# Order of the first loads: columns 2 and 3 of x third, the index table behind the last columns

## Chip, core and metric

The kernel runs on one core of a Trainium2 chip. Its time is the device time of one execution in microseconds (us). Before the change it takes 178.44 us, the median of 9 runs (178.29 to 178.66).

## What is computed

The reference, cut to what matters:

```python
x  = A_x                                   # 1 x 2048 x 512, bf16
xn = layernorm(x)                          # over the 512
fft   = irfft2(rfft2(xn) * (w_r + 1j*w_i))
geglu = (gelu(xn @ w_gate) * (xn @ w_up)) @ w_down    # 512 -> 1792 -> 512
return x + fft + geglu
```

## The kernel before

**Tiling.** The 2048 rows lie as 16 "columns" of 128 rows: column c holds rows 16p + c for partition p. Four columns make a block. The gate and up weights (512 x 1792) lie as four slices of 128 inner rows, the middle width as 14 tiles of 128 (f = 0 to 13).

**Order of the work.** Matrix work on TensorE (PE) is one long list: a gate group and an up group (L490; the first gate group of all is L498) for each unit of columns and f, between them the matmuls of the Fourier part (L577, L635, L644, L738, L768), then the down projection (L817, L821). The order on each engine is fixed when the kernel is built. A planner (class `Plan`, L135 to L198) sorts the operations by estimated costs and landing times (the tables `LAND`, `WG_LAND`, `WU_LAND`, L308 to L312). The hardware then runs each engine's list strictly in that order, and an instruction waits for its inputs by semaphores.

**The first microseconds.** PE spins on zeros (L320). Columns 0 and 1 are normalized on VectorE (DVE) one by one (statistics L339 and L342, normalization L345) and transposed on PE (L351). Then come, in this order on PE: six more spin matmuls (L324), the gate group of column 0 for f 0 to 3 (L498, needs the first third of the gate weights `Wg_sb`), the transposes of column 1, the up group of column 0 (L490, needs the first third of the up weights `Wu_sb`), gate and up of column 1, the gate group of columns 0 and 1 for f 4 and 5 (needs the second part of `Wg_sb`), the transposes of columns 2 and 3, and so on. Columns 2 and 3 are normalized together on DVE and GpSimd (POOL, L357 to L361) after their statistics.

**The loads.** All plain loads are issued by SyncE (SP), one after the other, on one DMA queue, in the order of lines L281 to L306. `load_x(c0, n)` (L272) loads n columns, 128 KB each; `load_w(T, a, b)` (L275) loads the columns a to b of all four slices of one weight. The first thirds are 512 KB each, the last parts 768 KB each. The index table `idx_t` (L283, L284) is 128 rows of 12 bytes; it is read only by GpSimd's indirect loads (`gather`, L593) late in the Fourier part. Loads share eight semaphores in turn, so that from the ninth load on each waits until the load eight places before it has landed. Behind the loads in SP's list stand the DMA transposes of xn (L455), which feed the gate and up groups of blocks 1 to 3.

Of the kernel before, what the change touches and what calls it, by code (L numbers as in the profile page):

```python
# [201 lines left out]
def kernel(  # L202
# [11 lines left out]
    nc = tc.nc  # L214
    const_np, ccols, rf_np, ri_np, idx_np = _tables()
# [32 lines left out]
    def load_consts(first, last):  # L248
        a, b = ccols[first][0], sum(ccols[last])
        nc.sync.dma_start(out=CT[:, a:b], in_=cap[:, a:b])  # L250


    def load_x(c0, n, eng=nc.sync):
        eng.dma_start(out=x_t[:, c0:c0 + n, :], in_=x_v[:, c0:c0 + n, :])

    def load_w(a, b, eng=nc.sync):
        nc.sync.dma_start(out=Wg_sb[:, :, a:b], in_=wg_v[:, :, a:b])
        eng.dma_start(out=Wu_sb[:, :, a:b], in_=wu_v[:, :, a:b])
# [21 lines left out]
    pin(nc.scalar.activation(out=warm[:], in_=eps_t[:], func=AF.Sqrt, bias=eps_t[:], scale=1.0))  # L280
    pin(load_x(0, 1))  # L281
    pin(load_x(1, 1))
    idx_t = pc.tile([P, 3], I32, name="idx_t")  # L283
    nc.sync.dma_start(out=idx_t[:], in_=nc.inline_tensor(idx_np, name="spec_rows").ap())  # L284
    load_w(Wg_sb, 0, 512)
    load_w(Wu_sb, 0, 512)
    load_x(2, 2)
    load_w(Wg_sb, 512, 1024)
    load_w(Wu_sb, 512, 1024)
    load_x(4, 2)  # L290
# [6 lines left out]
        nc.sync.dma_start(out=RF_t[:, c:c + 8], in_=rf_d.rearrange("p (c k) -> p c k", c=NC)[:, c:c + 8])  # L297
    load_x(12, 2)
    load_x(14, 2)
    load_consts("F0", "L0")  # L300
    load_consts("I0", "M0")
    for T, w_in in ((TR, A_w_r), (TI, A_w_i)):
# [578 lines left out]
```

## Time and profile before

The profiled execution took 178.44 us, as long as the median of the nine runs. Its span, from the first to the last recorded instruction, is 176.7 us; the rest (1.7 us) lies around it.

| engine | busy us | share of the span |
|---|---|---|
| PE, matmul | 172.3 | 97% |
| PE, weight load | 96.4 | 55% |
| DVE | 116.0 | 66% |
| ACT | 95.9 | 54% |
| POOL | 17.2 | 10% |

The first loads, from the trace's DMA issues and landings (us from the start of the span):

| load, in order of issue | size | issued | landed |
|---|---|---|---|
| x column 0 | 128 KB | 0.80 | 2.94 |
| x column 1 | 128 KB | 1.24 | 3.43 |
| idx_t | 1.5 KB | 1.71 | 3.76 |
| Wg_sb, first third | 512 KB | 2.18 | 6.16 |
| Wu_sb, first third | 512 KB | 2.65 | 7.63 |
| x columns 2 and 3 | 256 KB | 3.20 | 8.39 |
| Wg_sb, second part | 512 KB | 3.75 | 10.11 |
| Wu_sb, second part | 512 KB | 4.23 | 11.60 |

How to read it: "issued" is the start of the instruction on SP's queue, "landed" the moment at which the last of the 16 DMA engines reports its share as written. An engine that is busy for most of the span sets the time; another engine's idle time costs nothing as long as the busy one doesn't wait for it.

### The profile page before, as it was taken

To read this page: it belongs to the slowest core of one execution; us is meant where nothing else is said; L and a number is where in the kernel's file an instruction comes from. 1 tells how busy PE (TensorE), PEld (TensorE's weight loads), DVE (VectorE), ACT (ScalarE), POOL (GpSimd) and SP (SyncE) were. 2 spreads that over 40 slices of the span, in tenths; PEclk is the share of its full clock that TensorE was granted. 3 is DMA by queue.
4 is the path that set the end of the run, shared out by engine and by line. 5 is a ranking of instruction groups with operands and counts; after the bars stand their busy time and mean duration, and the time that the engine had idled before them with its cause. 6 is when DMAs were issued, how large, how long until landed. Compare 5 with 4: busy or idle time off the path is not lost.

```text
span 176.7 us, 3132 instructions
## 1 busy us (share of the span) xinstructions
PE 172.3 (97%) x1145; PEld 96.4 (55%) x1145; DVE 116.0 (66%) x255; ACT 95.9 (54%) x170; POOL 17.2 (10%) x38
## 2 busy tenths in 40 slices
PE   7899999999999999999999999999999999999993
PEld 7698845455545554555555445454444445444463
DVE  3578999987334699979899999643516325345333
ACT  4442489799736988898899965362112111211200
POOL 1020340506760000000000000000000000000000
PEclk9999999999999999999999999999999999999999
DMA  3999999233718702211201510200122222221212
GB/s 91 360 374 379 368 187 151 59 70 67 254 31 270 268 0 59 59 30 35 59 24 37 152 46 15 59 0 4 59 89 89 80 72 61 89 89 60 82 40 59
DMA packets 21871, 19.35 MB, mean 109 GB/s; under 512 B 8480, under 2 KB 20000, under 8 KB 21856
## 3 DMA queue, kind: packets, MB, share of 16 engines
q1 hardware_dynamic: 21440, 17.84, 36.3%
q0 software_dynamic: 416, 1.32, 2.4%
q8 instruction: 9, 0.15, 0.3%
q14 instruction: 6, 0.05, 0.1%
HBM read 13.38 MB, written 2.10 MB: 88 GB/s over the span
## 4 chain that ended last, share of the span: by engine, by line
PE 94%; DMA 3%; SPq 1%; issue 0%; DVE 0%
PE u_ps L490 28%; PE y_ps L817 27%; PE g_ps L490 27%; DMA Wu_sb<-in_B_w_up_dram 3%; PE dp L635 2%; PE yp L768 2%; PE gp L738 2%; PE bp L577 2%; PE y_ps L821 2%; PE ep L644 2%; SPq L273 0%; PE tp L351 0%; SPq L277 0%; SPq L284 0%; DVE y_sb L824 0%
## 5 line engine op out<-in xcount | busy, mean ns | idle before, releaser
L490 PE MATMUL u_ps<-xnT,Wu_sb 128*128 128x512 bf16 (+2 forms) x272 | 57.3, 341 | 0.2 <-DMA Wu_sb<-in_B_w_up_dram 0.2
L490 PE MATMUL g_ps<-xnT,Wg_sb 128*128 128x512 bf16 (+2 forms) x256 | 56.2, 349 | 0.0
L817 PE MATMUL y_ps<-Wd_sb,hT 128*128 128x512 bf16 (+2 forms) x252 | 51.1, 355 | 0.0
L508 DVE TENSOR_TENSOR hT<-u_ps,ge 128x512 bf16<-128x512 f32 x56 | 38.4, 688 | 18.2 <-PE u_ps L490 14.6
L503 ACT ACTIVATE ge<-g_ps 128x512 bf16<-128x512 f32 x56 | 33.7, 601 | 24.2 <-PE g_ps L490 23.3
L490 PEld LDWEIGHTS <-Wu_sb 128*128 128x128 bf16 x272 | 24.9, 98 | 21.0 <-DMA Wu_sb<-in_B_w_up_dram 0.4
L817 PEld LDWEIGHTS <-hT 128*128 128x128 bf16 x252 | 23.2, 98 | 22.4
L490 PEld LDWEIGHTS <-Wg_sb 128*128 128x128 bf16 x256 | 24.0, 98 | 20.6
L774 ACT CAST yf<-yp 128x512 bf16<-128x512 f32 x16 | 9.3, 586 | 40.5 <-PE yp L768 40.5
L824 DVE TENSOR_TENSOR y_sb<-y_ps,y_sb 128x512 bf16<-128x512 f32 (+2 forms) x18 | 11.1, 631 | 30.1 <-PE y_ps L821 30.1
L649 ACT CAST E<-ep 64x512 bf16<-64x512 f32 x32 | 18.5, 579 | 1.4 <-PE ep L644 1.0
L339 DVE BATCH_NORM_STATS2 stats<-x_t 128x6 f32<-128x512 bf16 x16 | 10.3, 672 | 2.4 <-DMA x_t<-in_A_x_dram 2.4
L452 ACT ACTIVATE xn<-x_t,nb,rstd 128x512 bf16<-128x512 bf16 x12 | 9.5, 812 | 1.0 <-POOL nb L370 1.0
L547 ACT CAST ds<-dp 128x512 bf16<-128x512 f32 x16 | 9.2, 597 | 0.8 <-PE dp L635 0.8
L547 ACT CAST Gs<-gp 128x512 bf16<-128x512 f32 x16 | 8.7, 591 | 0.6 <-PE gp L738 0.5
L547 ACT CAST Bs<-bp 128x512 bf16<-128x512 f32 x16 | 8.3, 608 | 0.5 <-PE bp L577 0.5
L780 DVE TENSOR_TENSOR lv<-yf 128x512 bf16<-128x512 bf16 x16 | 6.1, 421 | 1.5 <-ACT yf L774 0.6
L768 PEld LDWEIGHTS <-Gs 128*128 128x128 bf16 x64 | 4.8, 98 | 3.5
L787 DVE TENSOR_TENSOR yt<-lv 128x512 bf16<-128x512 bf16 x16 | 6.1, 421 | 0.3
L821 PE MATMUL y_ps<-yt,RI_t 128*128 128x512 bf16 (+2 forms) x18 | 6.1, 355 | 0.0
L768 PE MATMUL yp<-CT,Gs 128*128 128x128 bf16 x64 | 6.0, 219 | 0.0
L559 DVE TENSOR_TENSOR A<-xn 128x1024 bf16<-128x1024 bf16 x8 | 5.2, 676 | 1.0 <-ACT xn L452 1.0
(65 smaller groups left out, 118.5 us busy)
## 6 DMA issues: line engine op xcount, KB each, us to landing
F<-F SPq DMA_DIRECT2D x32, 64.0 KB, 2.0
y_sb<-in_A_x_dram SPq DMA_DIRECT2D x16, 128.0 KB, 2.1
out_dram<-y_sb SPq DMA_DIRECT2D x15, 128.0 KB, 1.7
x_t<-in_A_x_dram SPq DMA_DIRECT2D x7, 256.0 KB, 8.7
Wd_sb<-in_B_w_down_dram SPq DMA_DIRECT2D x1, 1792.0 KB, 7.4
Wg_sb<-in_B_w_gate_dram SPq DMA_DIRECT2D x2, 512.0 KB, 5.2
Wu_sb<-in_B_w_up_dram SPq DMA_DIRECT2D x2, 512.0 KB, 6.2
Wg_sb<-in_B_w_gate_dram SPq DMA_DIRECT2D x1, 768.0 KB, 10.1
```

Source lines behind the costliest of these rows:

```text
L339: V.bn_stats(out=st[:], in_=x_t[:, c, :])
L452: xn_op[c] = add("ACT", 0.72, lambda c=c: A.activation(out=xn[:, c, :], in_=x_t[:, c, :], func=AF.Identity, bias=nb[:, c:c + 1], scale=rst ...
L490: T_.matmul(b[name][:, f], lhsT=W_[:, e, (f0 + f) * P:(f0 + f + 1) * P], rhs=rhs[:, e, :], start=(e == 0), stop=(e == NE - 1))
L503: A.activation(out=b["ge"][:], in_=b["g_ps"][:], func=AF.Gelu_apprx_tanh)
L508: V.tensor_tensor(out=hT_of(sb, f0, m, o, w), in0=b["u_ps"][:], in1=b["ge"][:], op=ALU.mult)
L547: A.copy(out=o, in_=i)
L649: A.copy(out=b["E"][64 * h:64 * h + 64, r], in_=b["ep", h][64 * r:64 * r + 64])
L768: T_.matmul(t[:, q], lhsT=late["G"][:, q, c0 + j], rhs=IQ[q], start=(q == 0), stop=(q == 3), skip_group_check=True)
L774: A.copy(out=b["yf"][:, j], in_=b[j][:])
L817: T_.matmul(b[o][:], lhsT=hT_of(sb, f, 1, cl * P, P)[:, 0], rhs=Wd_sb[:, f, o:o + w], start=(f == 0), stop=False)
L821: T_.matmul(b[o][:], lhsT=late["RI"][:, c, :], rhs=late["yt"][:, c, o:o + w], start=False, stop=True)
L824: V.tensor_tensor(out=b["y"][:, o:o + w], in0=b[o][:], in1=b["y"][:, o:o + w], op=ALU.add)
```

## The change

Two lines of the loading order move. No instruction of PE, DVE, ACT or POOL is added, removed or put in another place.

```diff
     pin(load_x(0, 1))
     pin(load_x(1, 1))
+    load_x(2, 2)
     idx_t = pc.tile([P, 3], I32, name="idx_t")
-    nc.sync.dma_start(out=idx_t[:], in_=nc.inline_tensor(idx_np, name="spec_rows").ap())
     load_w(Wg_sb, 0, 512)
     load_w(Wu_sb, 0, 512)
-    load_x(2, 2)
     load_w(Wg_sb, 512, 1024)
     load_w(Wu_sb, 512, 1024)
     load_x(4, 2)
...
     load_x(12, 2)
     load_x(14, 2)
+    nc.sync.dma_start(out=idx_t[:], in_=nc.inline_tensor(idx_np, name="spec_rows").ap())
     load_consts("F0", "L0")
```

So x columns 2 and 3 (256 KB) stand third in SP's list, ahead of the first thirds of both weights. Every load from the second Wg_sb part to x columns 14 and 15 moves up one place in the turn of the eight semaphores, and the index table stands between x columns 14 and 15 and the constants.

## Prediction

> **What bounds the kernel now.** I read the page's table of engines first, then the chain that ended last, then PE's waits, and last the DMA by stretches of time.
>
> ```profile
> PE 172.3 (97%) x1145; PEld 96.4 (55%) x1145; DVE 116.0 (66%) x255; ACT 95.9 (54%) x170; POOL 17.2 (10%) x38
> ```
>
> PE is busy for 172.3 of 176.7 us. The chain in order of time (start, length) says where the rest is:
>
> ```profile
> 1.24 0.42 SPq L273
> 1.71 0.42 SPq L284
> 2.18 0.43 SPq L277
> 2.65 4.98 DMA Wu_sb<-in_B_w_up_dram
> 7.68 1.07 PE u_ps L490 x16
> ```
>
> Up to 7.68 us the end is set by SP issuing loads one by one and by the landing of the first third of Wu_sb (2.65 + 4.98 = 7.63 us). From 7.68 us on it is PE alone. PE's waits, in full:
>
> ```profile
> PE sp_ps L320 <- DVE minus_half L266: 1.1, 1, 1.1
> PE g_ps L498 <- DVE xn L345: 0.3, 1, 0.3
> PE u_ps L490 <- DMA Wu_sb<-in_B_w_up_dram: 0.2, 1, 0.2
> ```
>
> After the third wait there is none: PE has no idle stretch over 15 ns between 7.68 and 174.0 us. So the time of this kernel is the start of the first up group plus a fixed length of matmuls, and **the change is worth what it does to the landing of two loads**: the first third of Wg_sb (6.16 us, used at 6.20) and of Wu_sb (7.63 us, used at 7.68). PE's gap ahead of 6.20 is put down to xn L345 in the row above, but the weight load of the same group is listed with 0.5 us of waiting for Wg_sb, which came last.
>
> **What the change removes: nothing from PE.** VectorE waits for the moved columns:
>
> ```profile
> 8.42 1.29 DVE L339 BATCH_NORM_STATS2 stats<-x_t 128x6 f32<-128x512 bf16 x2 [0.46 <-DMA x_t<-in_A_x_dram]
> 12.11 0.61 PE L351 MATMUL tp<-ident_t,xn 128*128 128x128 bf16 x8
> ```
>
> These statistics can start 0.47 us earlier, when the copy of column 1 ends (7.53 + 0.42 = 7.95 us). But PE comes to the transposes of columns 2 and 3 only at 12.0 us, straight from the gate group before them, without a gap. I cost this gain at 0; PE's own list hides it, and after it PE is still what is late.
>
> **What it moves on SP.** Third place on SP goes from the index table (issue 0.42 us) to a 256 KB load (0.50 us in its old place, 0.33 to 0.50 elsewhere), so Wg_sb is issued 0 to 0.1 us later. The delay from issue to the first packet is 1.03 us for x column 0 (0.80 to 1.83), 1.06 for the index table, 1.09 for Wg_sb (2.18 to 3.27): Wg_sb's descriptors would be ready at 3.3 to 3.4 us. That is not when they run, for the same queue then still holds the 256 KB.
>
> **What it moves on the DMA engines.** This is the term that decides. The columns are the stretch, its length, busy time (instructions) of PE, PEld, DVE, ACT and POOL, the clock, the busy share of the 16 DMA engines, and GB/s:
>
> ```profile
> 2.50:3.00 0.50, 0.50 (x8) 0.50 (x6) 0.04 (x1) 0.00 (x0) 0.00 (x0) 1.00 0.81 223
> 3.00:3.25 0.25, 0.25 (x5) 0.25 (x3) 0.25 (x1) 0.00 (x0) 0.00 (x0) 1.00 0.11 10
> 3.25:3.75 0.50, 0.50 (x8) 0.50 (x6) 0.47 (x2) 0.00 (x0) 0.00 (x0) 1.00 0.82 72
> 3.75:4.25 0.50, 0.50 (x8) 0.50 (x6) 0.50 (x2) 0.30 (x1) 0.00 (x0) 1.00 0.50 98
> 4.25:5.00 0.75, 0.63 (x10) 0.46 (x9) 0.71 (x5) 0.00 (x0) 0.00 (x0) 1.00 1.04 367
> ```
>
> There is a **hole from 3.0 to 4.25 us**. x columns 0 and 1 are through at 3.0; the index table fills its place in the queue with 1.5 KB; Wg_sb begins at 3.27 and runs slowly for a microsecond. 18 of its packets there take over 150 ns, the longest 851, where 46 is usual; then it reaches 367 GB/s. Moved in the hole: 0.25 x 10 + 0.5 x 72 + 0.5 x 98 = 88 kB; at 367 GB/s it would be 1.25 x 367 = 459 kB. So 371 kB, or 371 / 367 = 1.01 us of the queue, goes unused. The moved load is 262 kB, or 262 / 367 = 0.71 us. Its first packet would be there at 1.71 + 1.06 = 2.77 us, before x column 1 is through, so it runs in the hole.
>
> The bounds for the landing of the two first thirds:
>
> - Best: the hole is filled whole. +0.71 for the load, -1.01 for the hole: **-0.30 us**.
> - Hand-over kept: the queue already shows the moved load followed by a weight in the same layout, where the second Wg_sb part runs behind x columns 2 and 3:
>
> ```profile
> 7.00:7.50 0.50, 0.49 (x9) 0.32 (x6) 0.00 (x0) 0.20 (x1) 0.00 (x0) 1.00 0.99 340
> 7.50:8.25 0.75, 0.57 (x11) 0.58 (x12) 0.42 (x1) 0.40 (x1) 0.00 (x0) 1.00 1.05 317
> ```
>
>   Against 367 these lose 0.5 x 27 + 0.75 x 50 = 51 kB, or 0.14 us; there is no hole. So -0.30 + 0.14 = **-0.16 us**.
> - Slow start kept: if Wg_sb's slow microsecond is its own and comes whenever it starts, the load still covers only the part up to 3.25. Wg_sb starts at 3.0 + 0.71 = 3.71 instead of 3.25: **+0.46 us**.
> - Worst: the load itself brings no cover, and all its 0.71 us come on top: **+0.71 us**.
>
> I take **-0.2 us**, between the first two, because the nearest row is the same pair of loads in the same order; and the first third of Wu_sb, as cold as Wg_sb, shows no hole either where it starts behind a full queue (5.00 to 5.50 us: 358 GB/s). Even Wd_sb, which starts into idle engines at 53.7 us, has 297 GB/s in its second half microsecond. A slow microsecond belongs to none of them.
>
> The Trainium skill speaks against the change: "DMA: Bandwidth & Descriptors", section "Queues, rings and completion order", says that each DMA engine consumes the descriptors of a ring in order, so that whatever is put ahead of a weight must be started before it. By that rule taken alone the sum would be the size of the load over the rate, the last bound above; the trace's hole at 3.0 to 4.25 us is what the rule leaves out.
>
> **From landing to the end.** If Wu_sb lands 0.2 us earlier, PE's first up group starts 0.2 us earlier, if Wg_sb also comes in time: it lands earlier by about the same. PE's floor: the six spin matmuls end at 5.90, then 16 gate matmuls (0.91 us from 6.20 to the transposes at 7.11) and the transposes of column 1 (four at 56 ns, 0.22 us): 7.03 us. So no more than 7.68 - 7.03 = 0.65 us can be gained, whatever the loads do. Next on PE is the second part of Wg_sb (landed 10.11, used at 10.37). The bytes ahead of it are the same in both orders, less the hole, so it comes up to 1.0 us earlier and doesn't bind. A late start goes to the end in full, for PE has nowhere to make it up.
>
> **The rest costs nothing, with its cover.** The index table late: SP issues it behind x columns 14 and 15, which land at 22.77 now; it is first used at 41.8 us, about 17 us of cover. Its small packets may open a hole there as early on; 1.0 us at most, ahead of the constants and twiddle loads (used from 41.8 us) and the DMA transposes behind them. The transposes of block 1 land by 29.80, and PE uses them at 32.71: 2.9 us of cover. The semaphores' turn: the first transpose (22.06 us) now waits for x columns 14 and 15 (22.77) instead of 12 and 13 (21.62); it stood behind the twiddle loads in the queue anyway and landed at 27.44. The loads from the ninth on wait for other landings, one place earlier or later, while the engines are full (357 to 397 GB/s from 8.25 to 20 us), so their order of service stays. Each of these costs 0 unless its cover is gone.
>
> **Rivals.**
>
> 1. Hole filled, small gain (forecast): 178.44 - 0.2 = 178.2 us, own range -0.30 to 0 (178.1 to 178.4). Chance 0.50.
> 2. Larger gain: the 12-byte rows are what stalls Wg_sb, and what they did to the slower DMA engines goes too. Wg_sb's shares finish from 5.64 to 6.16 us; if this spread of 0.5 us shrinks by half, 0.25 is added to the 0.2: 178.0 us, at most 0.65 less (177.8). For it: the slow packets follow those rows directly and nothing else in the trace. Against it: Wu_sb's shares spread as far (7.13 to 7.63). Chance 0.22.
> 3. Slower, one mechanism: Wg_sb's slow start is its own, and the 256 KB ahead only push it back. +0.46 gives 178.9 us, up to 179.15 at the worst bound. It decides from the point where more than 0.30 us of the slow start remains. For it: nothing in the trace shows this first touch of Wg_sb behind a full queue. Against it: the three starts named above. Chance 0.20.
> 4. Cancel: part of the slow start is kept (some 0.3 us), 178.4 to 178.7 us. Or the hole closes, but the load's packets run at the 223 to 258 GB/s of x columns 0 and 1: 262 / 240 = 1.09 instead of 0.71 us, so -0.16 + 0.38 = +0.22. Chance 0.08.
>
> That the change does not do what it says is excluded for the order on SP, which is the program's order; that the earlier columns help no one is part of the forecast.
>
> **The numbers.** The profiled execution took 178.44 us, the median itself, so the sum is made on both: 178.2 us. What a measurement of this kernel can tell from no change is about 0.2%, or 0.36 us. Faster by more: rival 2 but for its smallest values, 0.22. Slower by more: rival 3 and a little of 4, 0.22. Within: 0.56. The range takes in rival 2 to -0.6 and rival 3 to +0.5: 177.85 to 178.95 us.
>
> **What the profile after would show.** If right: no stretch under 200 GB/s between 2.25 and 8 us; x columns 2 and 3 landed before 4.6 us; Wg_sb's first third at about 5.95 and Wu_sb's at about 7.4; the first L490 group at 7.45; PE without a gap after it; the first statistics of column 2 at about 7.7 to 7.95 with no DMA wait. Rival 2: Wu_sb before 7.2. Rival 3: the slow stretch again, at 3.7 to 4.7, and Wu_sb after 8.0. The forecast would be wrong altogether if PE shows new gaps after 7.7 us, at the use of Wg_sb's second part or at 32.7 us behind the transposes.

## The result and the profile after

The changed kernel takes **179.5 us** (median of 10 runs, 179.15 to 180.8), the kernel before 178.44 (median of 30 runs, 178.29 to 178.98): a ratio of 1.006, 95% interval 1.0048 to 1.0071. So it is 1.06 us slower; the forecast was 178.2 us. The profiled execution after took 179.56 us with a span of 177.9, 1.12 us more than the one before.

The page's line of engines after the change. PE's busy time is the same to 0.1 us, so nothing was added to PE's work:

```profile
PE 172.4 (97%) x1145; PEld 96.7 (54%) x1145; DVE 115.9 (65%) x255; ACT 95.9 (54%) x170; POOL 17.2 (10%) x38
```

The chain that ended last, after the change (start, length):

```profile
1.71 0.42 SPq L273
2.14 0.04 issue
2.18 0.43 SPq L277
2.61 0.04 issue
2.66 6.10 DMA Wu_sb<-in_B_w_up_dram
8.76 0.05 issue
8.80 1.07 PE u_ps L490 x16
```

It is the same chain. The issue of `Wu_sb` is where it was (2.66, before 2.65); from there to its landing it took 6.10 us instead of 4.98. The first up group starts at 8.80 instead of 7.68, and PE's last matmul at 174.87 instead of 173.74: +1.12 at the start, +1.13 at the end, and no gap between. PE's waits, all of them:

```profile
PE g_ps L498 <- DMA Wg_sb<-in_B_w_gate_dram: 1.4, 1, 1.4
PE sp_ps L320 <- DVE minus_half L266: 1.1, 1, 1.1
PE u_ps L490 <- DMA Wu_sb<-in_B_w_up_dram: 0.2, 1, 0.2
```

The new one is the first: PE stands 1.4 us before the first gate group, for the first third of `Wg_sb`. PE's list at this place, before (first three rows) and after (start, length; in brackets the idle time ahead of it):

```profile
6.20 1.07 PE L498 MATMUL g_ps<-xnT,Wg_sb 128*128 128x128 bf16 x16 [0.31 <-DVE xn L345]
7.11 0.39 PE L351 MATMUL tp<-ident_t,xn 128*128 128x128 bf16 x4
7.68 1.07 PE L490 MATMUL u_ps<-xnT,Wu_sb 128*128 128x128 bf16 x16 [0.19 <-DMA Wu_sb<-in_B_w_up_dram]
7.31 1.07 PE L498 MATMUL g_ps<-xnT,Wg_sb 128*128 128x128 bf16 x16 [1.40 <-DMA Wg_sb<-in_B_w_gate_dram]
8.21 0.39 PE L351 MATMUL tp<-ident_t,xn 128*128 128x128 bf16 x4
8.80 1.07 PE L490 MATMUL u_ps<-xnT,Wu_sb 128*128 128x128 bf16 x16 [0.21 <-DMA Wu_sb<-in_B_w_up_dram]
```

Before, PE was idle for 0.31 us ahead of this gate group and for 0.19 ahead of the up group; now it is 1.40 and 0.21, together 1.11 us more. So both weights are late, and the chain names only the one that ended last: the transposes behind the gate group end at 8.60, so with `Wg_sb` this late the up group could not have started before that, however early `Wu_sb` had come. That is 0.92 us of the 1.12.

What the DMA engines did in that time (columns as in the prediction, the last is GB/s), first the kernel after the change:

```profile
2.50:3.00 0.50, 0.50 (x8) 0.50 (x6) 0.03 (x1) 0.00 (x0) 0.00 (x0) 1.00 0.98 275
3.00:3.25 0.25, 0.25 (x5) 0.25 (x3) 0.25 (x1) 0.00 (x0) 0.00 (x0) 1.00 0.82 238
3.25:3.75 0.50, 0.50 (x8) 0.50 (x6) 0.47 (x2) 0.00 (x0) 0.00 (x0) 1.00 1.02 231
3.75:4.25 0.50, 0.50 (x8) 0.50 (x6) 0.50 (x2) 0.29 (x1) 0.00 (x0) 1.00 0.70 129
4.25:5.00 0.75, 0.75 (x10) 0.70 (x9) 0.71 (x5) 0.00 (x0) 0.00 (x0) 1.00 0.75 205
```

The hole of before (10, 72 and 98 GB/s) is filled, but badly: the moved load runs at 231 to 275 GB/s, not 367, and **a slow stretch comes again** (129 and 205 GB/s from 3.75 to 5.0 us, where before had 367 after 4.25). The slow packets, those over 150 ns, are now spread: 10 from 2.5 to 3.5 us, 13 from 3.5 to 4.0, 7 from 4.0 to 4.5; the longest take 1147 and 1007 ns. The size of a packet tells whose it is: the moved load comes in 128 packets of 2 KB, `Wg_sb` in packets of 1 KB. Of the moved load's packets 23 are slow, and its last starts at 4.72 us; of `Wg_sb`'s 10 are slow up to 5.0 us, where before it was 18. So the stretch from 3.75 to 5.0 us is the tail of the moved load and the slow start of `Wg_sb` together.

A load has landed when the slowest of the 16 engines has its share. The moments of the shares, from the trace (us; "third" is the load that stands third in SP's list, and "median" here the ninth of the 16 shares):

| kernel | third: median / last | Wg_sb: median / last | Wu_sb: median / last |
|---|---|---|---|
| before | index table | 5.85 / 6.16 | 7.41 / 7.63 |
| before, second profile | index table | 5.86 / 6.11 | 7.33 / 7.69 |
| after | 4.36 / 5.10 | 6.32 / 7.26 | 7.84 / 8.76 |
| after, second profile | 4.34 / 5.65 | 6.44 / 7.08 | 7.92 / 8.56 |

Two terms are to be read here. The median share of `Wg_sb` comes 0.46 to 0.59 us later, about the 0.46 us of rival 3, though rival 3 reached its number with a moved load of 0.71 us. And `Wg_sb`'s last share lies 0.64 to 0.94 us behind the median instead of 0.25 to 0.31 (`Wu_sb`'s 0.64 to 0.92 instead of 0.22 to 0.36). The lag is passed on: after the change the last shares of the four weight loads in a row (7.26, 8.76, 10.27, 11.73) are all 0.9 us behind their medians. That slow packets on one engine hold back what is queued behind them there would do this; the trace does not say which engine a packet ran on, so it is an inference. No part of the prediction has this term. The second profiles (178.92 and 179.38 us) show the wide lag in both executions of the changed kernel, but not in the same form: in the first the last share is 0.50 us behind the next-to-last in `Wg_sb`, in the second 0.01. Nor is a late share the changed kernel's alone: in the second profile before, x columns 2 and 3 in their old place have theirs 1.06 us behind the median.

### The profile page after: what moved, and what is told of

Read it like the earlier page. It is cut to its first block, busy times and chain, and to the rows that moved or that the text cites. A ratio compares the mean times of both kernels' runs of the same rounds, so it can differ in the third digit from the quotient of the medians.

```text
span 177.9 us, 3133 instructions
## 1 busy us (share of the span) xinstructions
PE 172.4 (97%) x1145; PEld 96.7 (54%) x1145; DVE 115.9 (65%) x255; ACT 95.9 (54%) x170; POOL 17.2 (10%) x38
## 4 chain that ended last, share of the span: by engine, by line
PE 93%; DMA 3%; SPq 1%; issue 0%; DVE 0%
PE u_ps L490 27%; PE y_ps L817 27%; PE g_ps L490 27%; DMA Wu_sb<-in_B_w_up_dram 3%; PE gp L738 2%; PE bp L577 2%; PE yp L768 2%; PE dp L635 2%; PE y_ps L821 2%; PE ep L644 2%; SPq L273 1%; PE tp L351 0%; SPq L277 0%; DVE y_sb L824 0%
```

## The experiments

**Theories.** The expectations number what may make packets slow: the start of the first weight load as such (1); a fixed moment of the program (2); the index table's 12-byte rows (3); the layout of the load, 2 KB from each 16 KB as two adjacent rows of 1 KB, so early in the stream (4); columns 2 and 3 themselves (5); the first touch of the weights' addresses (6). Bytes alone, whatever their layout, are the plainest rival. My first account takes 1 and 4 together: the moved load stacks a slow load on a slow start. Unless said otherwise each ratio is against the kernel before on the same chip, with its 95% interval; there it took 178.47 to 178.76 us.

**The change in halves.** The index table alone late, x columns 2 and 3 in their old place; and the columns third, with the index table right behind them:

```diff
 idx_late, against before
-    nc.sync.dma_start(out=idx_t[:], in_=nc.inline_tensor(idx_np, name="spec_rows").ap())
     load_w(Wg_sb, 0, 512)
...
     load_x(14, 2)
+    nc.sync.dma_start(out=idx_t[:], in_=nc.inline_tensor(idx_np, name="spec_rows").ap())
 x23_third, against before
     pin(load_x(1, 1))
+    load_x(2, 2)
     idx_t = pc.tile([P, 3], I32, name="idx_t")
...
     load_w(Wu_sb, 0, 512)
-    load_x(2, 2)
```

> The index table alone goes behind x columns 14 and 15; columns 2 and 3 stay where they were before. Theory 1 (the slow start belongs to the first weight load, whenever it starts): Wg_sb's first third is issued 0.47 us earlier and can start at 3.0 instead of 3.27; Wu_sb lands 0.25 to 0.45 us earlier, 178.0 to 178.2 us. Theory 2 (the DMA engines are slow until some 4 to 5 us after the start, whatever they carry): Wu_sb lands at 7.4 to 7.7 as before, 178.3 to 178.5 us. Theory 3 (the 12-byte rows cause the stall): no stretch under 200 GB/s after 2.25 us, Wu_sb lands near 6.7 us, and PE's floor gives 177.8 us.

> Columns 2 and 3 alone go third; the index table follows them directly, ahead of both weights. Theories 1 and 2: as the changed kernel or up to 0.2 us more (one more issue ahead of Wg_sb), 179.4 to 179.7 us; the columns' shares again land over more than 1 us. Theory 3: the rows stall Wg_sb on top, 179.8 us or more.

The index table alone late: **178.09 us (177.93 to 178.48, 11 runs), ratio 0.9977 [0.9968, 0.9986]**. It beats both kernels. The columns third with the table behind them: 179.83 us (6 runs), 1.0075 [1.0058, 1.0093]. The kernel before took 178.47 beside these two; the 179.5 of the changed kernel was measured apart from them (178.44 before). So the table ahead of the weights costs 178.47 - 178.09 = 0.38 us with the columns in their old place and 179.83 - 179.5 = 0.33 with the columns third, and the columns third cost 179.5 - 178.09 = 1.41 and 179.83 - 178.47 = 1.36. The change is the sum of a gain of 0.4 and a loss of 1.4. The gain is shown by the times, not by the profile: the profiled execution of the first kernel was its slowest (178.48), with `Wu_sb` landed at 7.67. So by the time theory 1 was right and by the landing theory 2, and 179.83 is where theory 3 had put the other half. The profile does show that the 12-byte rows are not what makes `Wg_sb` start slowly. Without them, in the same stretches:

```profile
3.00:3.25 0.25, 0.25 (x5) 0.25 (x3) 0.25 (x1) 0.00 (x0) 0.00 (x0) 1.00 1.93 115
3.25:3.75 0.50, 0.50 (x8) 0.50 (x6) 0.47 (x2) 0.00 (x0) 0.00 (x0) 1.00 0.54 61
3.75:4.25 0.50, 0.50 (x11) 0.50 (x9) 0.50 (x2) 0.29 (x1) 0.00 (x0) 1.00 0.59 172
```

**Other loads in third place, index table late.** All move the index table as above and differ in what stands third: half of the table `RF_t` (256 KB, 2 KB from rows 4 KB apart, loaded here and no longer behind x columns 10 and 11; the expectation calls it contiguous, which it is not), column 2 alone, columns 4 and 5, columns 0 and 1 a second time, and the first 256 rows of x as one contiguous piece. The last two go into a tile that nothing reads.

```diff
 rf_third
+    nc.sync.dma_start(out=RF_t[:, 0:8], in_=rf_d.rearrange("p (c k) -> p c k", c=NC)[:, 0:8])
 x2_third (and load_x(3, 1) in the old place)
+    load_x(2, 1)
 x45_third (x columns 2 and 3 behind Wu_sb, as before; columns 4 and 5 no longer in their old place)
+    load_x(4, 2)
 x01_again
+    nc.sync.dma_start(out=again[:], in_=x_v[:, 0:2, :])
 flat_third
+    nc.sync.dma_start(out=again[:], in_=A_x.rearrange("b (h p r) d -> h p r (b d)", h=8, r=2)[0])
```

> In place of columns 2 and 3 another 256 KB load in 2 KB rows stands third: the first half of the forward table RF_t, which lies contiguously in memory; columns 2 and 3 stay behind Wu_sb's first third, the index table goes late as in the change. If the place in the queue is what costs (theories 1 and 2): Wu_sb lands within 0.2 us of the changed kernel's 8.76, 179.3 to 179.6 us. If the columns themselves are what is slow (rows 16 KB apart): RF_t's shares land within 0.5 us of each other, Wu_sb at 7.9 to 8.3, 178.7 to 179.1 us.

> Column 2 alone (128 KB) stands third, column 3 behind Wu_sb's first third, the index table late. If the cost goes with the bytes ahead of the weights: half of the changed kernel's 1.13 us, Wu_sb near 8.2 us, 178.9 to 179.1 us. If a third large load as such brings it: Wu_sb at 8.6 or later, 179.3 us or more. If only what exceeds the hole counts: Wu_sb at 7.4 to 7.7, 178.2 to 178.5 us.

> Columns 4 and 5 stand third instead of columns 2 and 3, which stay behind Wu_sb's first third; index table late. Same bytes, same row length and distance as in the changed kernel, other addresses. Theory 4 (what costs beyond the 0.46 us of the pushed slow start is the layout of the load, 2 KB out of every 16 KB): 179.3 to 179.6 us, the load's shares spread over about 1 us. Theory 5 (it is these two columns, next to the bytes of columns 0 and 1): 178.8 to 179.1 us, as with RF_t.

> Third stands a second load of columns 0 and 1 together (256 KB, 2 KB out of every 16 KB) into a tile that nothing reads; columns 2 and 3 stay behind Wu_sb's first third; index table late. The kernel moves 256 KB more than the others. If the slow packets come from the first touch of an address: these have just been read, so the load runs like RF_t and the time is 178.8 to 179.1 us. If the layout is what is slow: 179.3 to 179.6 us.

> As the run that loads columns 0 and 1 a second time, but the third load reads the first 256 rows of x in one piece of 256 KB (2 KB for each partition, one behind the other) into a tile that nothing reads. The kernel moves 256 KB more than the others. Same tensor, size, place and packet size; only the distance of the rows differs. Theory 4 (2 KB out of every 16 KB is what is slow): the shares land within 0.5 us of each other, Wu_sb at 7.8 to 8.2, 0.5 us or more under the run with columns 0 and 1 again: 178.8 to 179.3 us. If any x load at this place is slow: 179.6 to 180.3 us.

| third in the list | KB | rows apart | packets of it over 150 ns | Wu_sb's first third landed | time, ratio |
|---|---|---|---|---|---|
| index table (before, two profiles) | 1.5 | - | 0 | 7.63, 7.69 | 178.44 |
| nothing (idx_late) | 0 | - | - | 7.67 | 178.09, 0.9977 [0.9968, 0.9986] |
| half of RF_t | 256 | 4 KB | 4 of 128 | 7.83 | 179.0, 1.004 [1.002, 1.0061] |
| x, contiguous | 256 | none | 8 of 128 | 7.83 | 180.02, 1.0071 [1.0056, 1.0087] |
| x column 2 | 128 | 16 KB | not told apart | 7.92 | 179.18, 1.0043 [1.0027, 1.0059] |
| x columns 2 and 3 (after, two profiles) | 256 | 16 KB | 23, 19 of 128 | 8.76, 8.56 | 179.5, 1.006 [1.0048, 1.0071] |
| x columns 4 and 5 | 256 | 16 KB | 12 of 128 | 8.78 | 179.37, 1.0034 [1.001, 1.0058] |
| x columns 0 and 1 again | 256 | 16 KB | 23 of 128 | 8.65 | 180.25, 1.0104 [1.005, 1.0159] |

The landings fall in two groups. 256 KB from rows close together delay `Wu_sb` by 0.2 us, 256 KB from rows 16 KB apart by 0.9 to 1.1. So for the landing it is not the bytes, and not the first touch of an address, for columns 0 and 1 had been read a microsecond earlier. It is **the layout in this place**. The cleanest pair is the contiguous piece and columns 0 and 1 again: same tensor, size, place, packet size and target tile, 7.83 against 8.65 us. Each row but two rests on one profile; the two profiles of one kernel differ by up to 0.2 us. The times do not show the same groups: that pair has 180.02 and 180.25 us with overlapping intervals, `RF_t` 179.0 and columns 4 and 5 179.37. By its time the contiguous load is where "any x load at this place is slow" had put it (179.6 to 180.3), not where theory 4 had (178.8 to 179.3). Behind column 2 alone `Wu_sb` landed between two of its forecasts (7.4 to 7.7, and near 8.2): half the bytes in the 16 KB layout cost it 0.25 us, so the size counts too.

The contiguous load did not run well from the start. Eight of its first packets were slow (534 to 685 ns, at 3.0 to 3.2 us), then its shares landed within 0.3 us, and `Wg_sb`'s first packets came at 4.09 us, with 339 GB/s in the last row (the 383 of the row above are still mostly the contiguous load):

```profile
3.00:3.25 0.25, 0.25 (x5) 0.25 (x3) 0.25 (x1) 0.00 (x0) 0.00 (x0) 1.00 1.10 74
3.25:3.75 0.50, 0.50 (x8) 0.50 (x6) 0.47 (x2) 0.00 (x0) 0.00 (x0) 1.00 0.42 156
3.75:4.25 0.50, 0.50 (x8) 0.50 (x6) 0.50 (x2) 0.29 (x1) 0.00 (x0) 1.00 1.02 383
4.25:5.00 0.75, 0.75 (x10) 0.71 (x9) 0.71 (x5) 0.00 (x0) 0.00 (x0) 1.00 1.03 339
```

Here the slow stretch of `Wg_sb` is gone, which theory 1 did not expect: it does not come with `Wg_sb` wherever it starts. Behind half of `RF_t` it is there for half a microsecond (113 GB/s from 3.75 to 4.25, then 319).

The times of the kernels with close rows are higher than their landings say, for three other reasons. First, 256 KB more stand ahead of the second part of `Wg_sb` than before; at 367 GB/s they are 0.71 us, and before, that part landed at 10.11 and was used at 10.37. Second, slow packets turn up in columns 2 and 3 behind `Wu_sb` (188 GB/s from 7.5 to 8.0 us behind `RF_t`; some 45 slow packets from 7.0 to 9.5 us behind the contiguous piece). That is no property of these kernels: the second profile of the kernel before has 193 GB/s from 7.5 to 8.0, where the first has 311. PE's wait for the second part in the kernel with the contiguous load, which had it landed at 11.65:

```profile
PE g_ps L492 <- DMA Wg_sb<-in_B_w_gate_dram: 1.0, 1, 1.0
```

With `RF_t` the second part landed at 10.74, 0.63 us later than before, which the 256 KB alone would explain. Its group starts at 10.79 instead of 10.37, and those 0.42 us are its whole loss of 178.87 - 178.44 = 0.43 in the profiled execution (0.20 of them come from the late `Wu_sb`). The third reason is one load more (last section), which adds 0.44 us at the end in the kernels with column 2 alone, columns 0 and 1 again, and the contiguous piece. So the column-2 kernel lost 0.29 us on PE and 0.44 at the end.

**Weights first.** `Wg_sb` and `Wu_sb` ahead of all of x (a single run, index table late).

```diff
-    pin(load_x(0, 1))
-    pin(load_x(1, 1))
+    pin(load_w(Wg_sb, 0, 512))
+    pin(load_w(Wu_sb, 0, 512))
...
+    load_x(0, 1)
+    load_x(1, 1)
```

> Both first thirds of the weights ahead of all columns, index table late; columns 0 and 1 land late, so the time is over 181 us, and only the loads are of interest. Theory 1 (the slow start belongs to the first weight load): Wg_sb's first microsecond stays under 200 GB/s, 1.9 to 3 us, and Wg_sb lands at 4.6 to 5.0. Theory 2 (slow until 4 to 5 us whatever is loaded): slow until 4 us, Wg_sb lands after 5.2. If the slow start comes of the change from columns to weights: no slow start, Wg_sb's median share at 3.8 or earlier.

182.77 us. `Wg_sb`, now first of all, again has a slow first microsecond (102 and 109 GB/s from 2.0 to 3.0 us), and the columns of x from 6.0 to 8.5 us run at 285, 219, 174 and 254 GB/s. The slow start does not need x ahead of it, and columns of x in the 16 KB layout are slow later too.

**First touch of Wg_sb.** The ACT queue first reads 4 bytes of each of its 512 rows.

```diff
+    touch = pc.tile([P, NE, 2], BF16, name="touch")
+    pin(nc.scalar.dma_start(out=touch[:], in_=wg_v[:, :, 0:2]))
```

> The index table late; ahead of everything, from ACT's queue, 4 bytes of each of the 512 rows of Wg_sb's first third are loaded into a tile that nothing reads. Theory 6 (the slow start is the first touch of the addresses of the gate weights): Wg_sb's first microsecond behind columns 0 and 1 has no slow packets, Wu_sb lands at 6.6 to 7.1, 177.7 to 177.9 us. If it is not: as the run with the index table alone late, plus the touch's own cost, 178.1 to 178.5 us, slow packets from 3.0 to 4.2 us as there.

179.11 us, 1.0025 [1.001, 1.004], above both forecasts: it has one load more (0.44 us at the end), and x column 0 landed at 3.37 instead of 2.94 beside the touch. Nine slow packets from 3.0 to 3.5 us are still there and four more up to 4.25 (18 in this time with the index table alone late), and `Wg_sb` landed at 6.14 (6.01 with the index table alone late). A first touch, in this form, is not the cause.

**Wg_sb on a second queue.** ACT issues it beside SP's x columns 0 and 1.

```diff
+    pin(load_w(Wg_sb, 0, 512, nc.scalar))
...
-    load_w(Wg_sb, 0, 512)
```

> The index table late; Wg_sb's first third issued from ACT's queue at the start, beside columns 0 and 1 on SP. Theory 1: the slow start runs beside the columns; Wg_sb lands at 5.0 to 5.5, Wu_sb at 6.5 to 7.1, columns 0 and 1 later by up to 0.7 us, and PE's floor moves with them: 177.6 to 178.2 us. If the slow packets hold up the columns' packets in the same DMA engines: columns 0 and 1 land 1 us later or more, 178.5 us or more.

180.87 us, 1.0126 [1.0111, 1.0141], the second of the two forecasts. `Wg_sb` landed at 5.03, but it shares the engines with x: column 1 landed at 5.38 instead of 3.43. Column 1's landing now leads the chain, and PE waits for its normalization:

```profile
1.24 4.14 DMA x_t<-in_A_x_dram
...
7.96 1.66 PE g_ps L498 x16
```

The Trainium skill, "DMA: Bandwidth & Descriptors", section "Issuing engines are not separate DMA queues", says that loads of all issuing engines interleave on the same 16 DMA engines; column 1's 1.95 us agree.

**All loads later.** A VectorE memset of the first half of x's tile holds back the loads, for the kernels before and after. In the first form of the changed kernel (after_delayed) the loads were not held in order and the weights went ahead of x, so it did not test the question; in the second form every load is pinned.

```diff
+    nc.vector.memset(x_t[:, 0:8, :], 0.0)
     pin(load_x(0, 1))
     pin(load_x(1, 1))
...
-    load_w(Wg_sb, 0, 512)
+    pin(load_w(Wg_sb, 0, 512))
```

> The changed kernel with all loads held back by some 2 us: VectorE first clears columns 0 to 7, which the first load must wait for. The loads' order is the changed kernel's. Theory 2 (slow until a fixed moment of the program): columns 2 and 3 and Wg_sb run without slow packets, Wu_sb's first third lands under 5.6 us after its issue instead of 6.10. Theories 1, 4 and 5: the same picture, shifted: Wu_sb 6.0 to 6.2 us after its issue, the shares of columns 2 and 3 over more than 1 us.

> The kernel before, with all loads, in their order, held back by some 2 us: VectorE first clears columns 0 to 7, which the first load must wait for. Only its times from the first issue on are of interest. If the engines are slow until a fixed moment of the program, 4 to 5 us after the start: Wg_sb has no slow stretch, Wu_sb's first third lands under 6.3 us after the first load's issue. If not: as in the kernel before, 6.8 us after it, with a stretch under 150 GB/s.

> The changed kernel, held back in the same way. Fixed moment: Wu_sb's first third within 0.7 us of the held kernel before, the total up to 0.7 us above it. If not: it lands 0.9 to 1.2 us later than there, 7.8 to 8.0 us after the first issue, and the total is 0.9 to 1.2 us above it.

The first took 186.46 us; `Wg_sb`, again first in the queue, ran its first microsecond at 82 and 201 GB/s. In the second form the first load is issued 2.38 us later, and there is a slow stretch again: 48 and 47 GB/s from 5.5 to 6.5 us in the kernel before, 109 and 168 from 6.0 to 7.0 after the change. Before, held: 182.59 us (4 runs), `Wu_sb` landed 7.00 us after the first issue (6.83 without the hold). After, held: 183.47 us (4 runs, 182.09 to 183.96), 7.82 us after (7.96 without). The slow stretch moved with the loads, so it is no fixed moment of the program. `Wu_sb` lands 0.81 us later in the second than in the first, between the two forecasts (0.7 at most, 0.9 at least). The totals differ by 0.88 us, but they say little: the runs of the second spread over 1.9, and in its profile the granted clock is 0.50 from 7.9 to 14.7 us.

**Both kernels once more.** The unchanged files, for a second profile; their shares are in the table with the result.

> The kernel before, a second execution under the profiler: the last share of each of the first loads within 0.15 us of the next-to-last, Wu_sb at 7.4 to 7.7.

> The changed kernel, a second execution under the profiler. If the late last share belongs to the kernel: again 0.3 us or more behind the next-to-last in Wg_sb and Wu_sb. If it belongs to the execution: under 0.2 us, with Wu_sb still past 8.3 us because the median share is 0.4 us or more late.

By this measure, the last share against the next-to-last, the single late share belongs to the execution: after the change it is 0.01 us in both loads now, where the first profile had 0.50 and 0.45. What both profiles share is `Wu_sb` past 8.3 us and a last share 0.64 us or more behind the median. Before, `Wu_sb` landed at 7.69, and `Wg_sb` and `Wu_sb` had their last two shares within 0.15 us, but x column 1 (0.40 us) and x columns 2 and 3 (0.50) did not. There the second part of `Wg_sb` landed at 10.80, and its group started 0.47 us later than in the first profile. The kernel before, too, can lose 0.4 us to late shares.

## Why the prediction was wrong, step by step

- **Right: start of the first up group plus a fixed list.** +1.12 us there is +1.13 us at PE's last matmul and +1.12 in the profiled time. The most that could be gained was put too high at 0.65 us: PE's two waits ahead of that group (0.31 and 0.19) leave 0.50.
- **Right: VectorE's wait is worth nothing.** The statistics of columns 2 and 3 no longer wait for a load:

```profile
8.97 1.28 DVE L339 BATCH_NORM_STATS2 stats<-x_t 128x6 f32<-128x512 bf16 x2
```

  They were forecast 0.47 us earlier and start 0.55 us later than before (8.42), behind the copy of column 1, which PE's late gate group delays.
- **Right: the covers held.** The index table landed at 22.88 and is used at 42.9; the transposes of block 1 landed by 30.65 and are needed at 33.8 at the earliest; PE has no gap behind 8.80. (The cover of the index table was 41.8 - 22.77 = 19 us by the prediction's own figures, not 17; nothing hangs on it.)
- **Failed: "I take -0.2 us ... because the nearest row is the same pair of loads in the same order".** This step decides the result. The row at 7.0 to 8.25 us is the same pair in another place of the stream, and in third place `Wu_sb` lands 1.13 us later in the profile. Nor does that row hold from one execution to the next: in the second profile before it is 223 instead of 317 GB/s from 7.50 to 8.25. Two sizes in it were wrong. The moved load was priced at 367 GB/s, 0.71 us; by the median shares it took 4.36 - 3.24 = 1.12 us. I had named its rate (240 GB/s, 1.09 us) in rival 4, but there with a closed hole behind it. And a slow start of `Wg_sb` came on top, as in rival 3, though with fewer slow packets than before (10 instead of 18).
- **Failed: the worst bound.** "All its 0.71 us come on top" assumed the mean rate; the measured +1.13 (+0.87 in the second profiles) lies beyond it. What is missing is the spread of the shares: `Wu_sb`'s median came 0.43 us later and its last share a further 0.70 behind (0.59 and 0.28 in the second profiles). A bound for a landing needs the slowest share, not the mean rate.
- **Failed: the index table's place at nothing.** Its move alone is worth -0.33 to -0.38 us, as rival 2 had it in direction (0.25 plus 0.2); the loss of the other half hid it. Rival 2's mechanism is not what the runs show, for `Wg_sb` starts as slowly without the 12-byte rows; where the gain comes from is open.
- **Rival 3** had the side and the mechanism in part: the slow start is pushed back, and both of its signs came (a slow stretch at 3.7 to 4.7 us, `Wu_sb` after 8.0). Its claim that this start is `Wg_sb`'s own fell with the contiguous load.
- The Trainium skill's rule in the prediction, that what stands ahead in the ring is started first, would have given +0.71; the sign was right, and the layout's share of the loss, some 0.9 us against close rows (8.76 - 7.83), is not in it.

**What stays open:** why packets from rows 16 KB apart are so slow early in the stream, when columns 4 to 7 with the same layout run in a stretch of 360 to 397 GB/s, from 11 to 13 us, in the kernel before. Nor is third place the only slow one: in their old place columns 2 and 3 ran at 311 GB/s in one profile of that kernel and at 193 in the other. For the landing, bytes, a fixed moment, 12-byte rows and first touch are each refuted as the one cause. The Trainium skill, "DMA: Bandwidth & Descriptors", section "Latency and other measured facts", has rates that fall with the row pitch, from 207 GB/s at 512 KiB to 103 at 4 MiB; 16 KB is far below, and by itself would not explain the fast rows later. No run here separated the pitch from the age of the queue further, nor gave x another layout in HBM.

## What to carry to other kernels

A hole in the DMA rate is not free room: ask of the load that is to fill it how its own packets run in that place, and of the load behind whether its slow start goes away or only moves. Price a landing by its last share, not by the mean rate: here a lag of 0.9 us stayed through the loads behind. Look also at the loads further back, for what is put ahead of one weight stands ahead of the next as well. When a change moves two things, try each alone: here the half that looked like a by-product (the 1.5 KB table behind the weights) gains 0.4 us, and the other loses 1.4.

## What else the runs showed of the hardware

- **The end of the program depends on the number of loads.** From the start of PE's last matmul to the end of the span it takes 3.0 us before and after, but 3.44 in the four kernels with one DMA more (column 2 alone, columns 0 and 1 again, the contiguous piece, the touch). SP waits for its eight load semaphores one after the other at the end, some 65 ns each; before, the last store's semaphore (175.82) is the last in that row, and with one load more the turn shifts and it is the first.
- **A slow first gate group, and a clock that the profile does not record.** With `Wg_sb` on ACT's queue, PE had stood idle for 1.43 us before the transposes at 6.61, and the first gate group took 1.86 us instead of 1.07, with weight loads of 151 instead of 98 ns. The profiled execution of the kernel with columns 4 and 5 third shows the same (1.89 us, 151 ns); it took 180.44 us, where that kernel's median is 179.37. The windows of both give a clock of 1.00 there, but their traces hold no record of the clock before 9.44 us and none at all, and where no record is, 1.00 is printed. Where there is one, the same durations (151 ns; 1.91 and 1.89 us) stand at a clock of 0.50, with the weights first and in the changed kernel held back:

```profile
9.90:11.90 2.00, 2.00 (x21) 2.00 (x20) 0.22 (x1) 0.56 (x2) 0.00 (x0) 0.50 1.07 386
9.50:11.50 2.00, 1.93 (x19) 1.93 (x20) 0.00 (x0) 0.01 (x1) 0.00 (x0) 0.50 1.08 378
```

  So half the clock is the likely cause in the first two as well. After the change itself, with a wait of 1.4 us at the same place, the weight loads stayed at 98 ns; what decides it is open.
